# The tail of a transformer block's backward pass: the input gradient's sum and copy on ScalarE, and another order for the last group's wqkv gradient

## The chip, the cores and the metric

The kernel runs on one core of a Trainium2 chip. A core has TensorE for matrix products, VectorE, ScalarE and GpSimd for the rest, and SyncE, which here only issues DMAs. The metric is the device time of one execution in microseconds, as the median of several runs.

## The reference

A block with attention and a gated feed-forward part, side by side on one normalised input, and all its gradients. The sequence has 2048 rows of 448 values, 16 heads of 28, and a feed-forward width of 1792; inputs and outputs are bf16.

```python
def _A_ref(x, wqkv, wo):                      # attention, H = 16, Dh = 28
    qkv = (x @ wqkv).reshape(B, S, 3, H, Dh)  # -> q, k, v per head
    p = softmax(q @ k.T * Dh ** -0.5)
    return (p @ v).reshape(B, S, D) @ wo

def _B_ref(x, w_gate, w_up, w_down):
    return (silu(x @ w_gate) * (x @ w_up)) @ w_down

def _fwd_reference(...):
    xn = _layernorm(x, axis=-1)
    return x + _A_ref(xn, A_wqkv, A_wo) + _B_ref(xn, B_w_gate, B_w_up, B_w_down)

out, vjp = jax.vjp(_fwd_reference, A_x, A_wqkv, A_wo, B_w_gate, B_w_up, B_w_down)
return (out, *vjp(grad_out))
```

The last step of the backward pass concerns us. With g the gradient with respect to the normalised row xn, the gradient of the input row is `rstd * (g - mean(g) - xn * mean(g * xn)) + grad_out`: it needs two sums per row, of g and of g times xn.

## The kernel before

The order of all instructions is written out by hand: each engine executes its own instructions in the order in which the program lists them, and a framework adds the waits between engines. There are three stages.

The first stage runs the forward attention for four groups of four heads, and lets TensorE do feed-forward products in between. The second runs the backward attention in 512 units of a query tile and a key block; per unit ScalarE computes `E` (L808), VectorE `ds` (L814), and SyncE's queue transposes `ds` by DMA. In between it computes the output rows, the feed-forward's part of the input gradient (in two summands, into `pA_d` and `pB_d`), and the wqkv gradient of groups 0 to 2 (jobs of kind `dwq`).

The third stage, the tail (L849 to L905), is what the change touches. It has this order:

- DMA loads: `dy_t` (the whole output gradient, ScalarE's queue, L854), four loads of `pab` (the feed-forward's parts of the input gradient, two halves each of `pA_d` and `pB_d`, L858), and the first `dq_c` loads (L864), all on SyncE's queue but the first. A `dq_c` tile holds the gradients of q, k and v for two row tiles of 128 rows, 768 KB; there are three buffers, and `load_c(t // 2 + 2)` is issued ahead of every even row tile, behind the stores of the row tiles before it.
- The wqkv gradient of the last group, for four blocks `c` of its 448 rows (128, 128, 128 and 64). `dwq_mms` gives 64 products for each block: 32 for keys and values (`kvm`, L622, from `dkv_sp`), then 32 for queries (`qm`, L627, from `dq_sp`). `dwq_out` copies the block on ScalarE (L637), rearranges it in six GpSimd copies (L644) and stores it (L645). The last `dq_sp` half comes from the transposition (L757) of `dq_o` (L753), the very last result of the second stage.
- 16 row tiles of the input gradient. TensorE adds the two `pab` parts by an identity matrix (L880) and 12 products of `dq_c` with `wq` (L882) into one PSUM bank, `g_ps`. Three PSUM tiles named `sd` rotate over the wqkv blocks and these row tiles. Then, per row tile: VectorE copies `g_ps` to `g_sb` and sums it in the same pass (`s1`, L886); VectorE multiplies `g_sb` by `xn` and sums (`junk`, `s2`, L890); two operations on one value per row make `bb` (L894) and `cc` (L896); ScalarE computes `t1 = rstd * g_sb + bb` (L899); VectorE computes `t2 = xn * cc + t1` (L901; the profile prints both `t1` and `t2` as `t`); GpSimd adds `dy_t` (`dx`, L904); SyncE's queue stores (L905).

Of the kernel before, what the change touches and what calls it, by code (L numbers as in the profile page):

```python
# [9 lines left out]
ACT = mybir.ActivationFunctionType  # L10
ALU = mybir.AluOpType
AX = mybir.AxisListType
FP32 = mybir.dt.float32
BF16 = mybir.dt.bfloat16
# [4 lines left out]
D = 448  # L19
# [5 lines left out]
P = 128  # L25
NT = S // P
# [11 lines left out]
def kernel(  # L38
# [19 lines left out]
    pe, act, dve, pool, sp = nc.tensor, nc.scalar, nc.vector, nc.gpsimd, nc.sync  # L58
# [27 lines left out]
    rstd = const.tile([P, NT], FP32, name="rstd")  # L86
    rl_all = const.tile([P, NT, H], FP32, name="rl_all")
    xn_sp = const.tile([P, NT, DP], BF16, name="xn_sp")
# [40 lines left out]
    for c, (d0, dn) in enumerate(DCH):  # L129
        pool.tensor_copy(  # L130
            out=wq_sb[:dn, c].rearrange("p t g (hh r) -> p t (g hh) r", r=HP)[:, :, :, :DH],
            in_=wst[:dn, c, :].rearrange("p (t h d) -> p t h d", t=3, h=H))
# [4 lines left out]
    for hh in range(4):  # L137
        pool.dma_start(out=wo_pad[HP * hh:HP * hh + DH, :, :D], in_=wo_v[hh])
    dve.tensor_reduce(
        out=r_ones[:], in_=ident_f[:].rearrange("p (a b) -> p a b", b=HP)[:, :, 28:30],  # L140
# [49 lines left out]
    for b in range(5):  # L190
        if b < 4:
            bs = slice(4 * b, 4 * b + 4)
            for i in range(4):
                t = 4 * b + i
# [4 lines left out]
            for i in range(4):  # L199
                t = 4 * b + i  # L200
                dve.tensor_scalar(out=xn_sp[:, t, :D], in0=x_b[b][:, i, :],
                                  scalar1=mv[:, t, 0:1], scalar2=rstd[:, t:t + 1],
                                  op0=ALU.subtract, op1=ALU.mult)
# [4 lines left out]
        if b > 0:  # L208
            for tq in range(3):
                m = proj_unit(0, tq, b - 1, "act" if tq == 0 else "dve")  # L210
# [32 lines left out]
    for b in range(4):  # L243
        sp.dma_start_transpose(
            out=dyT[:, 4 * b:4 * b + 4].rearrange("p t c s -> p (t c) s"),
            in_=dy_sp[:, 4 * b:4 * b + 4, :].rearrange("p t d -> p (t d)"))
# [309 lines left out]
    ps_sd = cst.enter_context(tc.tile_pool(name="ps_sd", bufs=3, space=PSUM))  # L556
# [58 lines left out]
    def dwq_mms(g, c, ps):  # L615

        out = []
        lhs = lambda t: xn_sp[:, t, c * P:(c + 1) * P]

        def kvm(t):  # L620
            for hp in range(2):
                pe.matmul(ps[:, hp * P:(hp + 1) * P], lhsT=lhs(t), rhs=dsp[2 * g + hp][0][:, t, :],  # L622
                          start=(t == 0 and hp == 0), stop=(t == NT - 1), skip_group_check=True)

        def qm(t):
            for hp in range(2):
                pe.matmul(ps[:, 256 + hp * 64:256 + hp * 64 + 64], lhsT=lhs(t),  # L627
                          rhs=dsp[2 * g + hp][1][:, t // 8, t % 4, t % 8 // 4, :],
                          start=False, stop=(t == NT - 1), skip_group_check=True)
        for f in (kvm, qm):  # L630
            out += [lambda t=t, f=f: f(t) for t in range(NT)]
        return out

    def dwq_out(g, c, ps):
        d0, dn = DCH[c]
        o = outp.tile([P, 384], BF16, name="dwq_raw")
        act.copy(out=o[:], in_=ps[:, :384])  # L637
        z = outp.tile([P, 3, 4, DH], BF16, name="dwq_z")
        kv = o[:, :256].rearrange("p (h v j r) -> p h v j r", h=2, v=2, r=HP)
        for tq in range(3):  # L640
            for hp in range(2):
                src = (o[:, 256 + 64 * hp:320 + 64 * hp].rearrange("p (j r) -> p j r", r=HP) if tq == 0
                       else kv[:, hp, 2 - tq])
                pool.tensor_copy(out=z[:, tq, 2 * hp:2 * hp + 2, :], in_=src[:, :, :DH])  # L644
        pool.dma_start(  # L645
            out=out_2[d0:d0 + dn, :].rearrange("p (t c) -> p t c", t=3)[:, :, g * 4 * DH:(g + 1) * 4 * DH],
            in_=z[:dn].rearrange("p t h d -> p t (h d)"))

    def job_mms(i, ps):
        j = jobs[i]  # L650
        if j[0] == "dwq":
            return dwq_mms(j[1], j[2], ps)
        if j[0] == "y":
            t, x = chunk[i]
            out = []
            for n in range(NFC + G):
                rhs = (wo_pad[:, n, :D] if n < G else wtile["wd"][:, n - G, :])
                out.append(lambda n=n, rhs=rhs: pe.matmul(ps[:, :D], lhsT=t[:, n, :], rhs=rhs,  # L658
                                                          start=(n == 0), stop=False))
            out.append(lambda: pe.matmul(ps[:, :D], lhsT=ident_bf[:], rhs=x[:], start=False, stop=True))  # L660
            return out
        t = chunk[i]
        w = wtile[("wg", "wu")[j[1]]]
        return [lambda n=n: pe.matmul(ps[:, :D], lhsT=t[:, n, :], rhs=w[:, n, :],  # L664
                                      start=(n == 0), stop=(n == NFC - 1)) for n in range(NFC)]
# [106 lines left out]
    for k in range(N + 2 * UW):  # L772
# [36 lines left out]
        if 1 <= k <= N:  # L809
# [5 lines left out]
            if qi not in TQ:  # L815
                sp.dma_start_transpose(out=dsT[:, :, :, qi * P:(qi + 1) * P].rearrange("p j c q -> p (j c) q"),
                                       in_=DS[k - 1][:].rearrange("p j c -> p (j c)"))
# [8 lines left out]
        if pos == 1 and job:  # L826
            st["aux"] = ps_x.tile([P, 512], FP32, name="aux")
            fillers = job_mms(W, st["aux"])
# [20 lines left out]
    with ExitStack() as fin:  # L849
        ckf = fin.enter_context(tc.tile_pool(name="ckf", bufs=3))  # L850
        wk = fin.enter_context(tc.tile_pool(name="wk", bufs=3))
        one = fin.enter_context(tc.tile_pool(name="one", bufs=1))
        dy_t = one.tile([P, NT, D], BF16, name="dy_t")
        act.dma_start(out=dy_t[:], in_=dy_d)  # L854
        pab = [one.tile([P, NT, D], BF16, name=f"pab{i}") for i in range(2)]
        for i, src in enumerate((pA_d, pB_d)):
            for hf in range(2):
                sp.dma_start(out=pab[i][:, 8 * hf:8 * hf + 8, :], in_=src[:, 8 * hf:8 * hf + 8, :])  # L858
        dq_c = {}

        def load_c(ck):
            if ck < NT // 2:
                dq_c[ck] = ckf.tile([P, 3 * G, 2 * P], BF16, name="dq_c")
                sp.dma_start(out=dq_c[ck][:], in_=dqkv_d[ck])  # L864
        load_c(0)
        load_c(1)
        for c in range(4):
            ps = ps_sd.tile([P, 2, 512], FP32, name="sd")
            for f in dwq_mms(3, c, ps[:, 0, :]):
                f()  # L870
            dwq_out(3, c, ps[:, 0, :])
        wq = wtile["wq"]
        for t in range(NT):
            if t % 2 == 0:
                load_c(t // 2 + 2)
            cks = dq_c[t // 2]
            g_t = ps_sd.tile([P, 2, 512], FP32, name="sd")
            g_ps = g_t[:, 0, :D]
            for i in range(2):
                pe.matmul(g_ps, lhsT=ident_bf[:], rhs=pab[i][:, t, :], start=(i == 0), stop=False)  # L880
            for n in range(3 * G):
                pe.matmul(g_ps, lhsT=cks[:, n, (t % 2) * P:(t % 2 + 1) * P], rhs=wq[:, n, :],  # L882
                          start=False, stop=(n == 3 * G - 1))
            g_sb = wk.tile([P, D], FP32, name="g_sb")
            s1 = wk.tile([P, 1], FP32, name="s1")
            dve.tensor_scalar(out=g_sb[:], in0=g_ps, scalar1=1.0, scalar2=None, op0=ALU.mult, op1=ALU.add,  # L886
                              accum_out=s1[:])
            junk = wk.tile([P, D], FP32, name="junk")
            s2 = wk.tile([P, 1], FP32, name="s2")
            dve.scalar_tensor_tensor(out=junk[:], in0=g_sb[:], scalar=1.0, in1=xn_sp[:, t, :D],  # L890
                                     op0=ALU.mult, op1=ALU.mult, accum_out=s2[:])
            bb = wk.tile([P, 1], FP32, name="bb")
            cc = wk.tile([P, 1], FP32, name="cc")
            dve.scalar_tensor_tensor(out=bb[:], in0=s1[:], scalar=-1.0 / D, in1=rstd[:, t:t + 1],  # L894
                                     op0=ALU.mult, op1=ALU.mult)
            dve.scalar_tensor_tensor(out=cc[:], in0=s2[:], scalar=-1.0 / D, in1=rstd[:, t:t + 1],  # L896
                                     op0=ALU.mult, op1=ALU.mult)
            t1 = wk.tile([P, D], FP32, name="t1")
            act.activation(out=t1[:], in_=g_sb[:], func=ACT.Identity, scale=rstd[:, t:t + 1], bias=bb[:, 0:1])  # L899
            t2 = wk.tile([P, D], FP32, name="t2")  # L900
            dve.scalar_tensor_tensor(out=t2[:], in0=xn_sp[:, t, :D], scalar=cc[:, 0:1], in1=t1[:],  # L901
                                     op0=ALU.mult, op1=ALU.add)
            dx = wk.tile([P, D], BF16, name="dx")
            pool.tensor_tensor(out=dx[:], in0=t2[:], in1=dy_t[:, t, :], op=ALU.add)  # L904
            sp.dma_start(out=out1_d[:, t, :], in_=dx[:])  # L905
# [31 lines left out]
```

## Time and profile before

| what | before |
|---|---|
| median of 3 runs | 1739.35 us (1738.14 to 1739.54) |
| the profiled execution's own time | 1738.91 us |
| its span in the profile | 1737.1 us |
| busy share of the span: TensorE, VectorE, ScalarE, GpSimd | 87%, 63%, 72%, 23% |
| last `dq_o` on VectorE, the second stage's last result | 1653.98 us |
| first product of `dq_c` with `wq` | 1675.71 us |
| first `t1` and last `t1` on ScalarE | 1679.60 and 1729.04 us |
| end of the last `dx` on GpSimd | 1731.69 us |

Times are microseconds from the span's start, durations of single operations microseconds or nanoseconds. A timeline row has the start, the busy time, the engine, the line of the program, the operation, what it writes and reads, the shapes, and in brackets how long the engine was idle before it and whose end released it. The chain of waits is the work that ended last, followed back from the end: each piece is what the next one waited for. Busy shares are averages over the three stages; the tail is the last 5% of the span and has to be read by itself.

### The profile page before, as it was taken

The page shows a single profiled execution, that of the slowest core. Times are in us where ns is not written, and L with a number is a line of the kernel's source. Part 1 is how long each engine was busy: PE and PEld are TensorE (multiplying, and loading weights), DVE is VectorE, ACT ScalarE, POOL GpSimd, SP SyncE. Part 2 cuts the span into 40 slices and gives each one's busy share as a digit, 9 for nine tenths or more (in the row PEclk, how much of TensorE's full clock was granted, in tenths as well). Part 3 has the DMA queues.
Part 4 walks back from the last instruction along what each step waited for, and adds up shares of the span by engine and source line. Part 5 has one row for each costly group of instructions (what it writes and reads, how often), then busy time and mean ns, then how long its engine had stood idle before and what let it go on. Part 6 is the DMA issues. An engine that isn't in the chain of part 4 may idle for free.

```text
span 1737.1 us, 31931 instructions
## 1 busy us (share of the span) xinstructions
PE 1504.9 (87%) x12176; PEld 590.4 (34%) x12176; DVE 1103.0 (63%) x1402; ACT 1242.1 (72%) x1346; POOL 400.8 (23%) x664
## 2 busy tenths in 40 slices
PE   3799999999999998868888888888888888888885
PEld 2132333333233332223333334333334333433352
DVE  5365555565555454527777767777777777777726
ACT  2497888888777776637777767777777877777711
POOL 4132334343333342420001011110102101111122
PEclk9699999999899999889999989999999999999988
DMA  3794758775866585659999799998999999899873
GB/s 122 149 184 96 160 115 177 142 141 124 173 142 122 106 171 111 135 168 218 202 188 202 143 193 185 178 202 178 205 185 184 209 170 171 156 176 177 168 236 102
DMA packets 682153, 285.11 MB, mean 164 GB/s; under 512 B 637792, under 2 KB 651088, under 8 KB 682000
## 3 DMA queue, kind: packets, MB, share of 16 engines
q1 hardware_dynamic: 653616, 215.74, 65.9%
q0 software_dynamic: 25808, 64.30, 14.6%
q10 hardware_dynamic: 2576, 3.04, 0.6%
q8 instruction: 95, 1.56, 0.4%
q14 instruction: 58, 0.48, 0.1%
HBM read 67.34 MB, written 63.44 MB: 75 GB/s over the span
## 4 chain that ended last, share of the span: by engine, by line
PE 63%; ACT 16%; DMA 6%; DVE 6%; issue 6%; SPq 1%; POOL 1%; ACTq 0%; DVEq 0%; POOLq 0%
PE s_ps L531 9%; PE f_ps L339 9%; PE f_ps L313 8%; ACT E L808 7%; ACT dsT L722 7%; PE aux L664 5%; PE o_ps L511 4%; PE sd L793 4%; PE aux L735 4%; PE aux L658 3%; PE aux L721 3%; PE f_ps L157 3%; PE acc L694 3%; PE sd L803 2%; DMA dsT<-ds 2%
## 5 line engine op out<-in xcount | busy, mean ns | idle before, releaser
L814 DVE TENSOR_TENSOR ds<-sd,E 128x1024 bf16<-128x1024 f32 x512 | 624.3, 1223 | 231.1 <-PE sd L803 209.8
L808 ACT ACTIVATE E<-sd 128x1024 bf16<-128x1024 f32 x512 | 518.5, 1027 | 176.0 <-PE sd L803 153.9
L535 ACT ACTIVATE eT<-s_ps 128x1024 bf16<-128x1024 f32 x512 | 517.9, 1024 | 158.5 <-PE s_ps L531 153.0
L803 PE MATMUL sd<-KV,QD 32*128 32x512 bf16 x1024 | 202.4, 388 | 61.2 <-ACT E L808 60.2
L793 PE MATMUL sd<-KV,QD 32*128 32x512 bf16 x1024 | 201.9, 391 | 7.7 <-DMA KV<-kT_d 7.6
L694 PE MATMUL acc<-E,dOsp 128*32 128x512 bf16 x1024 | 204.4, 396 | 0.6 <-ACT dkv_o L700 0.5
L531 PE MATMUL s_ps<-qT,kT 32*128 32x512 bf16 x1024 | 204.7, 397 | 0.0
L694 PE MATMUL acc<-ds,Qsp 128*32 128x512 bf16 x1024 | 204.6, 396 | 0.0
L722 ACT COPY dsT<-aux 128x1024 bf16<-128x1024 bf16 x128 | 129.5, 1012 | 47.9 <-PE aux L721 46.2
L339 PE MATMUL f_ps<-xnT,wgu 128*128 128x512 bf16 x448 | 137.2, 404 | 24.7 <-DVE w_sb L365 12.9
L378 POOL DMA_DIRECT2D hd_d<-fT x168 | 126.9, 769 | 39.2 <-DVE fT L363 25.4
L531 PEld LDWEIGHTS <-kT 32*128 32x128 bf16 x1024 | 48.3, 91 | 204.2 <-issue 201.9
L664 PE MATMUL aux<-W,ck 128*128 128x448 bf16 x448 | 101.0, 353 | 14.2 <-ACT dsT L722 14.2
L313 PE MATMUL f_ps<-xn_sp,f_sp 128*128 128x448 bf16 x448 | 110.6, 356 | 0.0
L803 PEld LDWEIGHTS <-QD 32*128 32x128 bf16 x1024 | 66.5, 91 | 105.6 <-issue 101.9
L511 PE MATMUL o_ps<-eT,v_sp 128*32 128x512 bf16 x1024 | 102.0, 400 | 0.0
L709 POOL DMA_DIRECT2D dqkv_d<-dkv_o x64 | 39.1, 616 | 271.1 <-ACT dkv_o L700 271.0
L793 PEld LDWEIGHTS <-QD 32*128 32x128 bf16 x1024 | 48.3, 91 | 138.2 <-issue 122.9
L735 PE MATMUL aux<-dsT,Ksp 128*32 128x512 bf16 x1024 | 75.2, 387 | 22.4 <-ACT dsT L722 18.1
L694 PEld LDWEIGHTS <-dOsp 128*32 128x32 bf16 x1024 | 50.7, 93 | 118.8 <-issue 118.7
L721 PE MATMUL aux<-ident_bf,ds 128*128 128x128 bf16 x1024 | 80.3, 222 | 12.3 <-DVE dq_acc L750 6.9
L351 DVE SCALAR_TENSOR_TENSOR g<-t_sb,f_ps 128x512 f32<-128x512 f32 x56 | 38.4, 686 | 65.1 <-ACT t_sb L349 64.9
(129 smaller groups left out, 1731.1 us busy)
## 6 DMA issues: line engine op xcount, KB each, us to landing
hd_d<-fT POOLq DMA_DIRECT2D x168, 128.0 KB, 4.3
ck<-hd_d SPq DMA_DIRECT2D x32, 448.0 KB, 4.2
ck<-hd_d SPq DMA_DIRECT2D x16, 576.0 KB, 4.7
dsT<-ds SPq DMA_TRANSPOSE x384, 3.9
dq_c<-dqkv_d SPq DMA_DIRECT2D x8, 768.0 KB, 4.6
dqkv_d<-dkv_o POOLq DMA_DIRECT2D x64, 64.0 KB, 3.1
W<-wT_d SPq DMA_DIRECT2D x14, 224.0 KB, 3.9
out_dram<-dw_o POOLq DMA_DIRECT2D x28, 96.0 KB, 3.8
```

What stands on the lines that cost most here:

```text
L313: pe.matmul(acc[:, :D], lhsT=src[:, 12 * (t // 4) + 4 * wi + t % 4, :], rhs=rhs[:, t, :D], start=(t == 0), stop=(t == NT - 1))
L339: pe.matmul(st[name][:], lhsT=w(c), rhs=src[:, tsl, c, :], start=(c == 0), stop=(c == 3))
L511: pe.matmul(o_ps[HP * hh:HP * (hh + 1), :], lhsT=v[:, kt, HP * hh:HP * (hh + 1)], rhs=e[hh // 2][:, hh % 2, :], start=(kt == 0), stop=(kt ...
L531: pe.matmul(s_ps[:, j, :], lhsT=kT[r:r + HP, kt * P:(kt + 1) * P], rhs=qT[r:r + HP, qc * 512:(qc + 1) * 512], start=True, stop=True, tile_ ...
L535: act.activation(out=e[:], in_=s_ps[:], func=ACT.Exp, scale=SCALE)
L664: return [lambda n=n: pe.matmul(ps[:, :D], lhsT=t[:, n, :], rhs=w[:, n, :], start=(n == 0), stop=(n == NFC - 1)) for n in range(NFC)]
L694: pe.matmul(acc[r:r + HP, :], lhsT=src[:, qt, 64 * hp + HP * j:64 * hp + HP * j + HP], rhs=m[:, j, :], start=(qt == 0), stop=(qt == NT - 1 ...
L722: act.copy(out=dsT[:, :, :, qi * P:(qi + 1) * P].rearrange("p j c q -> p (j c) q"), in_=ps[:])
L793: pe.matmul(s_ps[:, j, :], lhsT=q[HP * j:HP * j + HP, qt * P:(qt + 1) * P], rhs=kv[HP * j:HP * j + HP, kc * 512:(kc + 1) * 512], start=Tru ...
L803: pe.matmul(d_ps[:, j, :], lhsT=q[r:r + HP, qt * P:(qt + 1) * P], rhs=kv[r:r + HP, kc * 512:(kc + 1) * 512], start=True, stop=True, tile_p ...
L808: act.activation(out=E[k][:], in_=s_ps[:], func=ACT.Exp, scale=SCALE)
L814: dve.tensor_tensor(out=DS[k - 1][:], in0=d_ps[:], in1=E[k - 1][:], op=ALU.mult)
```

## The change

The wqkv gradient of the last group: `dwq_mms` returns the keys' and values' products and the queries' products as two lists. The tail first runs the keys' and values' products of all four row blocks, then the queries' products block by block, each followed by its `dwq_out`. For that the four blocks lie two by two in the two banks of two `sd` tiles, where each block had its own `sd` tile before. The jobs in the second stage keep their order.

The input gradient: the pass that copies and sums `g_ps` goes from VectorE to ScalarE (an Identity activation with `accum_out`), and its copy `g_sb` is bf16. `junk` and `t1` read `g_ps` in PSUM instead of `g_sb`. VectorE has 16 instructions fewer in the program's order and ScalarE 16 more; DMAs, products and GpSimd's work stay the same in number.

```diff
         for f in (kvm, qm):
-            out += [lambda t=t, f=f: f(t) for t in range(NT)]
+            out.append([lambda t=t, f=f: f(t) for t in range(NT)])
         return out
...
         if j[0] == "dwq":
-            return dwq_mms(j[1], j[2], ps)
+            return sum(dwq_mms(j[1], j[2], ps), [])
...
         load_c(0)
         load_c(1)
+        mms = []
         for c in range(4):
-            ps = ps_sd.tile([P, 2, 512], FP32, name="sd")
-            for f in dwq_mms(3, c, ps[:, 0, :]):
-                f()
-            dwq_out(3, c, ps[:, 0, :])
+            if c % 2 == 0:
+                g_t = ps_sd.tile([P, 2, 512], FP32, name="sd")
+            mms.append((g_t[:, c % 2, :], dwq_mms(3, c, g_t[:, c % 2, :])))
+        for part in range(2):
+            for c, (ps, m) in enumerate(mms):
+                for f in m[part]:
+                    f()
+                if part == 1:
+                    dwq_out(3, c, ps)
...
-            g_sb = wk.tile([P, D], FP32, name="g_sb")
+            g_sb = wk.tile([P, D], BF16, name="g_sb")
             s1 = wk.tile([P, 1], FP32, name="s1")
-            dve.tensor_scalar(out=g_sb[:], in0=g_ps, scalar1=1.0, scalar2=None, op0=ALU.mult, op1=ALU.add,
-                              accum_out=s1[:])
+            act.activation(out=g_sb[:], in_=g_ps, func=ACT.Identity, accum_out=s1[:])
             junk = wk.tile([P, D], FP32, name="junk")
             s2 = wk.tile([P, 1], FP32, name="s2")
-            dve.scalar_tensor_tensor(out=junk[:], in0=g_sb[:], scalar=1.0, in1=xn_sp[:, t, :D],
+            dve.scalar_tensor_tensor(out=junk[:], in0=g_ps, scalar=1.0, in1=xn_sp[:, t, :D],
                                      op0=ALU.mult, op1=ALU.mult, accum_out=s2[:])
...
-            act.activation(out=t1[:], in_=g_sb[:], func=ACT.Identity, scale=rstd[:, t:t + 1], bias=bb[:, 0:1])
+            act.activation(out=t1[:], in_=g_ps, func=ACT.Identity, scale=rstd[:, t:t + 1], bias=bb[:, 0:1])
```

## The prediction

> **What bounds the kernel now.** The change lies wholly in the tail, after the last attention gradient, so the page was read first for its end: the span is 1737.1 us, this execution's own time 1738.91 us (1.81 us lie outside the span), and the median of the three runs, 1739.35 us, is 0.44 us more. The sum below is made against 1738.91. About 0.2%, 3.5 us, is what a measurement can tell from no change.
>
> The second view is the chain of waits that ended last, where the tail begins.
>
> ```profile
> 1659.07 16.60 DMA dq_c<-dqkv_d
> 1675.66 0.05 issue
> 1675.71 2.46 PE sd L882 x12
> 1678.17 0.02 issue
> 1678.19 0.64 DVE g_sb L886 x2
> ```
>
> The first `dq_c` load takes 16.60 us because it queues behind `dy_t` and four `pab` loads, with the DMA engines full. TensorE stands waiting when it lands. The timeline of TensorE shows that the wqkv gradient ends before that:
>
> ```profile
> 1653.88 3.26 PE L622 MATMUL sd<-dkv_sp,xn_sp 128*128 128x128 bf16 x32
> 1662.36 0.96 PE L627 MATMUL sd<-dq_sp,xn_sp 128*128 128x64 bf16 x15 [4.74 <-DMA dq_sp<-dq_o]
> 1663.13 3.60 PE L622 MATMUL sd<-dkv_sp,xn_sp 128*128 128x128 bf16 x32
> ...
> 1672.13 1.10 PE L627 MATMUL sd<-dq_sp,xn_sp 128*128 128x64 bf16 x32
> 1673.07 0.54 PE L880 MATMUL sd<-pab,ident_bf 128*128 128x448 bf16 x2
> 1675.71 2.44 PE L882 MATMUL sd<-W,dq_c 128*128 128x448 bf16 x12 [2.10 <-DMA dq_c<-dqkv_d]
> ```
>
> There are two holes: 4.74 us for the last `dq_sp` transposition, and 2.10 us for `dq_c`. Only the second is on the path.
>
> Then the 16 tiles follow. VectorE's timeline, with those of ScalarE and GpSimd, gives one period:
>
> ```profile
> 1690.14 0.69 DVE L901 SCALAR_TENSOR_TENSOR t<-xn_sp,cc,t 128x448 f32<-128x448 bf16 x1 [0.83 <-ACT t L899]
> 1690.74 0.62 DVE L886 TENSOR_SCALAR_CACHE_REDUCE g_sb<-sd 128x448 f32<-128x448 f32 x1
> 1691.40 1.02 DVE L890 SCALAR_TENSOR_TENSOR junk<-g_sb,xn_sp 128x448 f32<-128x448 f32 x1
> 1692.35 0.15 DVE L894 SCALAR_TENSOR_TENSOR bb<-s,rstd 128x1 f32<-128x1 f32 x1
> 1693.45 0.69 DVE L901 SCALAR_TENSOR_TENSOR t<-xn_sp,cc,t 128x448 f32<-128x448 bf16 x1 [0.83 <-ACT t L899]
> ```
>
> ```profile
> 1692.60 0.76 ACT L899 ACTIVATE t<-g_sb,bb,rstd 128x448 f32<-128x448 f32 x1 [2.55 <-DVE bb L894]
> ```
>
> ```profile
> 1690.91 1.03 POOL L904 TENSOR_TENSOR dx<-t,dy_t 128x448 bf16<-128x448 f32 x1 [2.28 <-DVE t L901]
> ```
>
> VectorE is a ring: `t2` to `g_sb` 0.60, `g_sb` to `junk` 0.66, `junk` to `bb` 0.95, `bb` to `t1` on ScalarE 0.25, `t1` to `t2` 0.85; sum 3.31 us. From the first `t1` (1679.60) to the last (1729.04) it is 49.44 us for 15 periods. TensorE needs 2.65 us per tile (1678.37 to 1681.02) and is ahead. So VectorE with its wait for ScalarE sets the tail.
>
> `junk` is the row to look at. In the first tile, with GpSimd idle, it took 0.62; here `dx` runs from 1690.91 to 1691.94, and `junk` ends 0.48 after `dx`. It is held, not slowed. `g_sb`, which reads PSUM, overlaps `dx` too and keeps its 0.62.
>
> **The change, part by part.** (1) VectorE loses `g_sb`: 0.66 per period. ScalarE gets it. A plain ScalarE copy of 128x448 out of PSUM to bf16 took 0.527 (`row_o`, L673). What writing out the sum adds is in no row: VectorE's own read of its sum took 0.08, the smallest ScalarE operation (128x4, L197) 0.30, and no cost is the bound below. I take 0.15, between the two, so 0.68 with it. Nobody reads the new bf16 `g_sb`.
>
> (2) In the changed program's waits, `junk` waits for ScalarE, not for TensorE: the two passes over the same sums run one after the other. Here a rule speaks against the change. The Trainium skill, PSUM — Partial Sum Buffer, "PSUM bank collisions raise a hardware error", says that two engines must not read one bank at a time, so the pass that went to ScalarE can't lie beside `junk`; no run here shows a collision. By it the first tile gives the +0.06 below; side by side it would be about -0.5, and the sum 1733.4 instead of 1734.0.
>
> In steady state most of it hides. ScalarE starts it when `t1` of the tile before ends, while VectorE runs `t2`. From a `t1` start: 0.76, then 0.68, then 0.05 to `junk`, 1.49; VectorE is free at 0.85 + 0.60 = 1.45. So 0.04 shows. Were it not hidden, it would cost 0.73 a period. Queued behind `g_sb` on ScalarE is only its own tile's `t1`, which must wait for `junk` anyhow; behind the waiting `junk` on VectorE are `bb`, `cc` and `t2` of the same tile.
>
> In the first tile it shows fully: 0.04 + 0.68 + 0.05 + 0.55 + 0.19 = 1.51 from TensorE's end to `t1`, against 1.45 now. +0.06, between -0.09 and +0.21.
>
> (3) `junk` now reads PSUM and one SBUF tile. Bounds: 0.62 as alone, or held by `dx` as now. I take 0.62: `ds` (L814) has just these kinds of operands and took 1.23 us at 1037.80, across GpSimd's copies of 1037.47 to 1038.54, as it does without them.
>
> (4) `bb` and `cc` keep two SBUF inputs, and now start earlier, inside `dx`. Free, the ring is 1.49 + 0.55 + 0.25 = 2.29, less than TensorE's 2.65. Held, they go at the end of `dx`: from there 0.18 to `t1` (the short value of `bb` to `t1`, as part of `bb` is done by then), 0.85 to `t2`, 0.77 to `dx`, 1.03 for `dx`: 2.83. No row shows a 128x1 operation under `dx`; the nearest is `junk` itself, the same instruction with both inputs in SBUF, which is held. I take 2.83. The skill's page SBUF — State Buffer, "Who interferes with whom", makes no exception for small operands: two SBUF inputs contend with a GpSimd instruction that reads SBUF. By it the sum is 1734.0, by the bare 0.15 of the `bb` row 1731.5.
>
> `t1` out of PSUM I leave at 0.76; a lower bound is 0.59 (`t_sb`, 128x512 out of PSUM), by which TensorE's 2.65 would rule.
>
> (5) 15 periods: the first three have `t1` to `t2` 0.06 shorter (fewer waits), so 3 x 2.77 + 12 x 2.83 = 42.27. Gain 49.44 - 42.27 = 7.17.
>
> (6) The reordered gradient. The keys' and values' parts run through the 4.74 us hole: 1653.88 + 3.26 + 3 x 1.95 gives 1663.0, after `dq_sp` landed (1662.36). Then four queries' parts of about 1.0, of which the second and fourth wait some 0.6 for ScalarE's copy of the other half of their tile: done near 1668.4 instead of 1673.1. What hides it: `dq_c` lands at 1675.66 as before, since SP issues the same loads in the same order. GpSimd's copies and stores of the four blocks (84 KB each) come at most some 4 us earlier; at the 400 GB/s of that stretch each is 0.2 us of DMA, so `dq_c` moves by no more than 0.4. The gain is nothing; the wait grows from 2.1 to over 7 us.
>
> And that wait costs. The windows view shows the granted clock:
>
> ```profile
> 1660.00:1663.40 3.40, 1.04 (x18) 1.03 (x18) 0.00 (x0) 0.00 (x0) 0.00 (x0) 0.51 1.12 367
> 1663.40:1666.80 3.40, 3.40 (x37) 3.40 (x35) 0.00 (x0) 0.48 (x1) 1.79 (x7) 0.50 1.01 402
> 1666.80:1670.20 3.40, 3.40 (x90) 3.40 (x88) 0.00 (x0) 0.48 (x1) 1.48 (x7) 0.99 1.03 411
> ```
>
> Each row has the stretch, its length, busy time and count of TensorE, its weight loads, VectorE, ScalarE and GpSimd, then the clock, the DMA share and GB/s. After the 4.74 us hole it was 0.50, and back at 0.99 some 4.5 us after work began. After the 2.10 us hole it stayed at 1.00. Now the hole in front of `dq_c` is the long one, with one or two `pab` products in it, so tile 0 starts at half clock. Price, from the same rows: 15 queries' products 0.96 instead of 0.52, 32 of 3.60 instead of 1.95, 32 of 1.26 instead of 1.10: 2.25 us. On tile 0 it is fully on the path. Bounds: 0, and 3.4 if the half clock lasts 6.8 us.
>
> Sum: -7.17 + 0.06 + 2.25 = -4.86, 1738.91 - 4.86 = 1734.0.
>
> `dq_c` for later tiles is issued behind the store of `dx` two tiles back: 0.45 + 4.6 to land + two tiles of products 5.1 + 3.9 to the end of `dx` = 14.1 for six tiles, against 6 x 2.83 = 17.0: hidden, until landing takes 7.5.
>
> **The rivals.** *TensorE becomes the bound*: `bb` and `cc` aren't held (or `t1` is quicker), period 2.65. 49.44 - 15 x 2.65 = 9.69; -9.69 + 2.31 = -7.4, 1731.5. For it: they are 128x1. Against: the held `junk`.
>
> *The clock holds*: -2.25 off either, 1731.8 or 1729.3. Against: both idle stretches of 3 us or more (before 1652.05 and 1662.36) were followed by half clock.
>
> *Slower: `junk` still collides with `dx`*, though one input is in PSUM. It now starts within 0.1 us of `dx`. If `junk` is first, `dx` starts at 1.49 + 0.55 = 2.04 and ends at 3.07, `bb` is held till then: 3.25. If `dx` is first (1.62 to 2.65), `junk` ends 0.48 later: 2.65 + 0.48 + 0.25 = 3.38. Over 15 periods -0.9 or +1.1, with the 2.31 of the start: 1740.3 to 1742.3, and 1743.5 with the longer half clock. It decides from a period of 3.15 up. Against it: `g_sb` and `ds` rows.
>
> *The reorder alone does what the words say*: impossible as a gain while `dq_c` lands at 1675.66; it is inside the sum at zero.
>
> **How the numbers follow.** Forecast 0.50, 1734.0, with own bounds 1731.8 (no half clock) to 1735.2. TensorE's bound 0.22, 1731.5. Clock holds 0.10, 1729.3 to 1731.8. `junk` collides 0.10, 1740.3 to 1743.5. Left, 0.08: late `dq_c` and the unseen, around 1737 to 1740. The range from 1729.0 to 1737.0 leaves out `junk`'s collision and most of the rest. Faster by over 0.2% (under 1735.9) 0.79, within 0.2% 0.14, slower 0.07.
>
> **What would show it.** `junk` at 0.62 in all tiles; `bb` and `cc` ending just after `dx`; `t1` starts 2.83 apart; over 7 us with only `pab` products before tile 0; clock 0.50 after 1675.7. I'm wrong if `junk` stays at 1.0, if the ring is 2.65 or over 3.1, if `dq_c` lands earlier, or if tile 0's products take 2.4 us.

## The result and the profile after

The changed kernel takes 1730.32 us (median of 22 runs, 1725.21 to 1739.99), the kernel before in the same sessions 1737.39 us (22 runs, 1731.33 to 1744.15). The ratio is 0.9963, 95% interval 0.9949 to 0.9978: faster by 0.2 to 0.5%. The forecast of 1734.0 stands for a ratio of 1734.0 / 1738.91 = 0.9972, inside the interval, and 1730.32 lies in its range of 1729.0 to 1737.0. The medians differ by 7.07 us.

The profiled execution took 1725.21 us with a span of 1723.4 us, 13.7 us less than the one before. This is not all the change's work: the last `dq_o` on VectorE, ahead of everything that was changed, already ends at 1647.24 instead of 1654.67 us, 7.43 us earlier. Over the fourteen profiled executions of this study, whose programs are all alike up to there, that end lies anywhere from 1647.24 to 1656.61 us. So the profiles are compared from that point on. I call the stretch from the end of the last `dq_o` to the end of the last `dx` the tail: 77.02 us before, 70.75 us after, a gain of 6.27 us. A second pair of profiles of the two kernels gave 77.78 and 70.61 us, a gain of 7.17 us. So the tails alone account for the difference of the medians, and the 7.43 us ahead of them are the scatter of single executions.

The chain of waits that ended last, after, at the start of the row tiles:

```profile
1652.11 16.71 DMA dq_c<-dqkv_d
1668.82 0.04 issue
1668.86 4.21 PE sd L888 x12
```

The first `dq_c` load is as long as before (16.71 against 16.60), and the 12 products behind it take 4.21 us where they took 2.46. TensorE's timeline has the reorder and its price:

```profile
1646.45 7.32 PE L622 MATMUL sd<-dkv_sp,xn_sp 128*128 128x128 bf16 x128
...
1659.25 1.09 PE L627 MATMUL sd<-dq_sp,xn_sp 128*128 128x64 bf16 x32 [0.64 <-ACT dwq_raw L637]
...
1664.57 0.53 PE L886 MATMUL sd<-pab,ident_bf 128*128 128x448 bf16 x1 [4.03 <-DMA pab<-pB_d]
1668.86 4.21 PE L888 MATMUL sd<-W,dq_c 128*128 128x448 bf16 x12 [3.77 <-DMA dq_c<-dqkv_d]
```

All 128 products of keys' and values' parts now run in one piece, and the last queries' part waits 0.64 us for ScalarE's copy of the other half of its tile. TensorE is done with the wqkv gradient at 1660.3, and then stands for 4.03 and 3.77 us with one `pab` product in between. The windows view has the granted clock as the third number from the end (before the DMA share and GB/s), here for two microseconds out of tile 0 and tile 1:

```profile
1671.00:1672.00 1.00, 1.00 (x4) 0.44 (x3) 0.00 (x0) 0.00 (x0) 0.00 (x0) 0.50 0.12 49
1673.00:1674.00 1.00, 1.00 (x7) 0.50 (x6) 0.22 (x1) 0.64 (x2) 0.00 (x0) 1.00 0.00 0
```

Four products in a microsecond at clock 0.50, seven at 1.00: tile 0 runs at half clock, tile 1 at full.

One late period, from the timelines of VectorE, ScalarE and GpSimd:

```profile
1710.74 0.68 DVE L906 SCALAR_TENSOR_TENSOR t<-xn_sp,cc,t 128x448 f32<-128x448 bf16 x1 [0.85 <-ACT t L904]
1711.34 0.62 DVE L895 SCALAR_TENSOR_TENSOR junk<-sd,xn_sp 128x448 f32<-128x448 f32 x1
...
1711.88 0.67 DVE L899 SCALAR_TENSOR_TENSOR bb<-s,rstd 128x1 f32<-128x1 f32 x1
1712.47 0.14 DVE L901 SCALAR_TENSOR_TENSOR cc<-s,rstd 128x1 f32<-128x1 f32 x1
```

```profile
1709.91 0.72 ACT L904 ACTIVATE t<-sd,bb,rstd 128x448 f32<-128x448 f32 x1 [1.48 <-DVE cc L901]
1710.54 0.53 ACT L892 ACTIVATE g_sb<-sd 128x448 bf16<-128x448 f32 x1
1710.96 0.20 ACT L892 ACTIVATION_READ_ACCUMULATOR g_sb<-sd 128x1 f32 x1
1712.64 0.72 ACT L904 ACTIVATE t<-sd,bb,rstd 128x448 f32<-128x448 f32 x1 [1.48 <-DVE cc L901]
```

```profile
1711.50 1.03 POOL L909 TENSOR_TENSOR dx<-t,dy_t 128x448 bf16<-128x448 f32 x1 [1.70 <-DVE t L906]
```

`junk` is back at 0.62 although `dx` runs from 1711.50 to 1712.53. `bb`, on one value per row, takes 0.67 and ends at 1712.55, 0.02 after `dx`: it is held. So it goes in every tile from the fifth on: `bb` starts ever earlier inside `dx`, its length grows from 0.15 in the first tile to 0.67, and it ends within 0.02 of `dx`'s end. The new ring goes through GpSimd: `dx`'s end to `t1` 0.11, `t1` to `t2` 0.83, `t2` to `dx` 0.76, `dx` 1.03, together 2.73 us against 3.31 before.

### The profile page after: what moved, and what is told of

Same layout as the page of the kernel before. It is cut to its first block, busy times and chain, and to the rows that moved or that the text cites. A ratio compares the mean times of both kernels' runs of the same rounds, so it can differ in the third digit from the quotient of the medians.

```text
span 1723.4 us, 31944 instructions
## 1 busy us (share of the span) xinstructions
PE 1494.2 (87%) x12176; PEld 586.3 (34%) x12176; DVE 1092.3 (63%) x1370; ACT 1251.4 (73%) x1378; POOL 400.8 (23%) x664
## 3 DMA queue, kind: packets, MB, share of 16 engines
q10 hardware_dynamic: 2576, 3.04, 0.6%
## 4 chain that ended last, share of the span: by engine, by line
PE 61%; ACT 16%; DMA 7%; DVE 6%; issue 5%; SPq 2%; POOL 1%; ACTq 0%; DVEq 0%; POOLq 0%
PE s_ps L531 9%; PE f_ps L313 8%; PE f_ps L339 8%; ACT E L808 7%; ACT dsT L722 7%; PE aux L664 5%; PE o_ps L511 4%; PE sd L793 4%; PE aux L735 4%; PE aux L658 3%; DMA dsT<-ds 3%; PE f_ps L157 3%; PE aux L721 3%; PE acc L694 2%; PE sd L803 2%
```

## The experiments

The theory: the gain is the shorter ring, held up by `dx` over `bb`; the reorder brings nothing and costs the half clock at tile 0; what sets the start of the tiles is the `dq_c` load. The rivals: the reorder has a share in the gain; the clock would have dropped anyway; the ring's length comes from something else than `dx`. All times in the table are from the profiles, in us; ratios are against the kernel before. "Start" is the time from the last `dq_o`'s end to the first `dq_c` product, "tile 0" the duration of its 12 products, "ring" the mean of the last five periods. In brackets are the names of the runs, by which the expectations call them.

| kernel | ratio, 95% interval | tail | start | tile 0 | ring |
|---|---|---|---|---|---|
| before | 1 | 77.02 | 21.04 | 2.44 | 3.31 |
| before, second profile | | 77.78 | 21.78 | 2.44 | 3.31 |
| after | 0.9963, 0.9949 to 0.9978 | 70.75 | 21.62 | 4.21 | 2.73 |
| after, second profile | | 70.61 | 21.63 | 4.08 | 2.73 |
| ScalarE part alone (`e1_scalar_only`) | 0.9949, 0.9931 to 0.9968 | 71.31 | 22.29 | 3.79 | 2.73 |
| reorder alone (`e2_reorder_only`) | 0.9998, 0.9980 to 1.0015 | 80.01 | 21.86 | 4.61 | 3.31 |
| `bb`, `cc` with one data input (`e3_free_small`) | 0.9955, 0.9935 to 0.9974 | 73.11 | 24.97 | 3.95 | 2.65 |
| `junk` from SBUF (`e4_junk_sbuf`) | 0.9979, 0.9964 to 0.9995 | 77.95 | 23.32 | 4.66 | 3.04 |
| TensorE kept busy (`e5_warm`) | one run, 1727.62 | 71.36 | 24.04 | 2.43 | 2.73 |
| `dq_c` ahead of half the `pab` (`e6_loads`) | 0.9914, 0.9890 to 0.9937 | 65.88 | 16.84 | 3.72 | 2.73 |
| the same, without reorder (`e7_loads_noreorder`) | 0.9922, 0.9905 to 0.9940 | 66.88 | 19.53 | 2.43 | 2.73 |
| `e6_loads`, `dy_t` late, free `bb` (`e9_loads_dy`) | 0.9902, 0.9882 to 0.9923 | 62.02 | 13.68 | 2.43 | 2.65 |
| and a third `dq_c` early (`e10_best`) | 0.9884, 0.9862 to 0.9905 | 60.44 | 13.26 | 2.43 | 2.65 |
| the last without reorder (`e11_best_oldorder`) | 0.9881, 0.9858 to 0.9903 | 58.98 | 12.08 | 2.44 | 2.65 |

### The two parts, each alone

The first kernel is the one before with the ScalarE edits only:

```diff
-            g_sb = wk.tile([P, D], FP32, name="g_sb")
+            g_sb = wk.tile([P, D], BF16, name="g_sb")
...
-            dve.tensor_scalar(out=g_sb[:], in0=g_ps, scalar1=1.0, scalar2=None, op0=ALU.mult, op1=ALU.add,
-                              accum_out=s1[:])
+            act.activation(out=g_sb[:], in_=g_ps, func=ACT.Identity, accum_out=s1[:])
...
-            dve.scalar_tensor_tensor(out=junk[:], in0=g_sb[:], scalar=1.0, in1=xn_sp[:, t, :D],
+            dve.scalar_tensor_tensor(out=junk[:], in0=g_ps, scalar=1.0, in1=xn_sp[:, t, :D],
...
-            act.activation(out=t1[:], in_=g_sb[:], func=ACT.Identity, scale=rstd[:, t:t + 1], bias=bb[:, 0:1])
+            act.activation(out=t1[:], in_=g_ps, func=ACT.Identity, scale=rstd[:, t:t + 1], bias=bb[:, 0:1])
```

> The kernel before with ScalarE's sum and copy alone; the wqkv gradient keeps its old order. Tail here means from the end of the last dq_o on VectorE to the end of the last dx on GpSimd: 77.0 us before, 70.75 us after. Theory (the ring gives the gain, the reorder costs a start at half clock): the ring is 2.73 us as after, tile 0's 12 products take 2.44 us and not 4.21, so the tail is 68.4 to 69.2 us, some 1.8 us less than after. Rival (the reorder helps or is free): the tail is 70.7 us or more.

The second is the one before with the reorder only:

```diff
...
-            for f in dwq_mms(3, c, ps[:, 0, :]):
-                f()
-            dwq_out(3, c, ps[:, 0, :])
...
+        for part in range(2):
+            for c, (ps, m) in enumerate(mms):
+                for f in m[part]:
+                    f()
+                if part == 1:
+                    dwq_out(3, c, ps)
```

> The kernel before with the reordered wqkv gradient alone; VectorE keeps sum and copy. Theory: dq_c lands as before, TensorE waits over 7 us for it, tile 0 starts at half clock, the ring is 3.31 us; the tail is 78.5 to 79.5 us, 1.5 to 2.5 us slower than before, about 0.1% of the time. Rival (the hole of 4.74 us was worth something): the tail is 77.0 us or less.

The ScalarE part alone has the whole gain (0.9949 of the time before) and the same ring of 2.73 us; the reorder alone has none that can be told (0.9980 to 1.0015). That settles where the gain comes from. The reorder alone has a tail of 80.01 us, 0.5 more than expected. That is 3.0 longer than before: 2.17 from tile 0 at half clock, 0.82 from a later start. But the ScalarE part alone did not get the tail of 68 to 69 us that the theory wanted. It got 71.31, which by the number is on the rival's side. Its TensorE timeline and windows say why:

```profile
1672.06 3.79 PE L882 MATMUL sd<-W,dq_c 128*128 128x448 bf16 x12 [2.33 <-DMA dq_c<-dqkv_d]
```

```profile
1672.00:1673.00 1.00, 0.94 (x5) 0.51 (x6) 0.00 (x0) 0.00 (x0) 0.00 (x0) 1.00 1.01 417
1673.00:1674.00 1.00, 1.00 (x4) 0.45 (x3) 0.00 (x0) 0.00 (x0) 0.51 (x4) 0.50 0.70 272
```

The order of the kernel before, and a wait of only 2.33 us, and the clock still falls to 0.50, about a microsecond after TensorE has begun again. So the half clock is not the reorder's alone, and the rival isn't needed for the 71.31: with tile 0 at 2.44 and no slow start of tile 1 (the first period is 2.99, against 2.66 in the changed kernel) the tail would have been 69.6, and the start was 0.67 later than in the changed kernel. The reorder makes the wait for `dq_c` 8 us instead of 2, and the half clock came with it every time instead of now and then.

To see how often that happens without a change, both unchanged kernels were profiled once more.

> The kernel before, unchanged, for a second profiled execution. In the first the clock stayed at 1.00 after the hole of 2.10 us, while in e1_scalar_only, which has the same order of loads and products up to tile 0, it fell to 0.50 for 3 us after a hole of 2.33 us. If the half clock depends on the reorder alone, tile 0's products take 2.44 us here; if it comes by chance of timing, 2.4 to 4.2 us. The tail by dq_c's landing alone is 77 to 81 us.

> The changed kernel, unchanged, for a second profiled execution: ring 2.73 us, tile 0's products 3.9 to 4.7 us at half clock, dq_c's first product 21 to 25 us after dq_o, tail 70 to 74 us.

The kernel before waited 1.66 us for `dq_c` this time (2.10 before) and again kept its clock, 2.44 us for tile 0; the changed kernel needed 4.08. With the loads as they are in these two, every kernel with the reorder paid it (3.95 to 4.66 in five profiles), and without the reorder one of three did.

The traces show what decides. In all fourteen, every stretch between two steps of the granted clock is a whole multiple of 3.41 us (10.24 us at half clock in the changed kernel, from 1662.25 to 1672.49), so the steps lie on a grid, in another place in each execution. The windows view over single stretches of that grid, for the holes in question:

| profile | stretch of the grid, us | TensorE busy in it | clock in the next |
|---|---|---|---|
| before, hole of 2.10 | 1673.70 to 1677.11 | 1.40 | 1.00 |
| before, second profile, hole of 1.66 | 1674.13 to 1677.55 and 1677.55 to 1680.96 | 2.60 and 2.57 | 1.00 |
| ScalarE part alone, hole of 2.33 | 1669.58 to 1672.99 | 1.08 | 0.50 |
| after | 1658.84 to 1662.25 | 1.28 | 0.50 |
| after, second profile | 1661.79 to 1665.20 | 1.39 | 0.50 |

Of the stretches at full clock that lie wholly in the tails of the fourteen profiles, the same limit divides all: after 1.39 us busy or less the next one is at 0.50, after 1.40 or more at 1.00. (It is a limit for these products; earlier in the program, with products of other shapes, the clock fell after a stretch with 2.18 us busy, 1636.59 to 1640.00 in the second profile of the kernel before.) So the length of the hole isn't what counts, but how it lies on the grid: 1.66 us were cut in two and harmless, and the kernel before kept its clock by a hundredth of a microsecond. The clock comes back at a step of the grid too, and the price is half of the time that the products run until then: in the changed kernel (1672.49 - 1668.86) / 2 = 1.8, measured 1.77.

### Does idling lower the clock?

The changed kernel, with 20 products of no use (into a tile of their own) after each of tile 0's two `pab` products, while it waits for `pab` and `dq_c`:

```diff
                 pe.matmul(g_ps, lhsT=ident_bf[:], rhs=pab[i][:, t, :], start=(i == 0), stop=False)
+                if t == 0:
+                    warm = ps_x.tile([P, 512], FP32, name="aux")
+                    for _ in range(20):
+                        pe.matmul(warm[:, :D], lhsT=ident_bf[:], rhs=xn_sp[:, 0, :D], start=True, stop=True)
```

> The changed kernel with 40 products of 128x448 that nobody reads (20 after each of tile 0's two pab products) to keep TensorE busy while it waits for dq_c. Theory (the idle stretch lets the clock fall): the clock stays at 1.00, tile 0's 12 products take 2.44 us and not 4.21, and from the first product of dq_c to the first t1 it is 3.9 us and not 5.66; the rest as after, so some 1.8 us less. Rival (the products of tile 0 are slow for another reason, such as the DMA traffic or late weights): 4.2 us as after. If dq_c lands earlier than in the other runs, the products before it may push tile 0 by up to some us.

```profile
1672.82 2.43 PE L892 MATMUL sd<-W,dq_c 128*128 128x448 bf16 x12
```

Tile 0 is at full clock, and from the first `dq_c` product to the first `t1` it takes 3.87 us instead of 5.66. The idling is the cause: the kernels of the next sections whose tile 0 follows other products without a wait have it at 2.43 or 2.44 too. In the tail as a whole it doesn't show (71.36), because the products of no use were themselves too many: the first `dq_c` was issued at 1653.70 and landed 16.7 us later, at 1670.4, 21.6 after `dq_o` as in the changed kernel, but the last of the 20 products ran until tile 0 began at 1672.82. That took back 2.4 us, more than the clock gave. The expectation had named this case.

### What holds the ring: the small operations, and `junk`

In the next kernel `bb` and `cc` take `rstd` as a scalar per row, not as a second data input:

```diff
-            dve.scalar_tensor_tensor(out=bb[:], in0=s1[:], scalar=-1.0 / D, in1=rstd[:, t:t + 1],
-                                     op0=ALU.mult, op1=ALU.mult)
+            dve.tensor_scalar(out=bb[:], in0=s1[:], scalar1=rstd[:, t:t + 1], scalar2=-1.0 / D,
+                              op0=ALU.mult, op1=ALU.mult)
```

> The changed kernel, with bb and cc as tensor_scalar: rstd is a per-partition scalar operand, so each has one tensor input in SBUF and not two. Theory (two SBUF inputs are what dx holds): bb takes 0.15 us in all tiles, the ring is under 2.65 us, TensorE sets the tile rate, t1 starts are 2.65 us apart; tail 69.6 us, 1.1 us less than after. Rival (bb is held for another reason, or any small operation is held): bb up to 0.67 us as after, ring 2.73 us, tail 70.7 us.

Its VectorE and GpSimd timelines:

```profile
1718.31 0.21 DVE L899 TENSOR_SCALAR bb<-s,rstd 128x1 f32<-128x1 f32 x1
```

```profile
1717.55 1.03 POOL L909 TENSOR_TENSOR dx<-t,dy_t 128x448 bf16<-128x448 f32 x1 [1.61 <-DVE t L906]
```

`bb` now starts and ends inside `dx` (1717.55 to 1718.58) in 0.21 us, in every tile, and the ring is 2.65, TensorE's own time per tile. So it was `dx` that held `bb`, through the second data input, and the first rival of the prediction is what happens without that hold. The tail didn't reach the 69.6 us expected, it is 73.11, since `dq_c` started 24.97 us after `dq_o` in this execution. The ring by itself is worth little: the last `t1` comes 40.07 us after the first, 0.78 less than in the changed kernel, and the interval of the ratio overlaps that of the changed kernel.

The other test gives `junk` its second SBUF input back:

```diff
-            dve.scalar_tensor_tensor(out=junk[:], in0=g_ps, scalar=1.0, in1=xn_sp[:, t, :D],
+            dve.scalar_tensor_tensor(out=junk[:], in0=g_sb[:], scalar=1.0, in1=xn_sp[:, t, :D],
```

> The changed kernel, but junk reads ScalarE's bf16 g_sb in SBUF instead of PSUM, so it has two SBUF inputs. Theory (dx holds what has two SBUF inputs, or is held by it): junk and dx collide in full, ring 3.2 to 3.4 us, tail 77 to 80 us, so nearly all of the gain is gone. Rival (taking g_sb off VectorE gave the gain, where junk reads from makes no difference): ring 2.73 us, tail 70.7 us.

The timeline of VectorE and GpSimd together:

```profile
1692.19 0.62 DVE L895 SCALAR_TENSOR_TENSOR junk<-g_sb,xn_sp 128x448 f32<-128x448 bf16 x1
...
1692.35 1.35 POOL L909 TENSOR_TENSOR dx<-t,dy_t 128x448 bf16<-128x448 f32 x1 [1.70 <-DVE t L906]
...
1692.73 0.98 DVE L899 SCALAR_TENSOR_TENSOR bb<-s,rstd 128x1 f32<-128x1 f32 x1
```

Here `junk` starts first and keeps its 0.62; it is `dx` that is held, 1.35 instead of 1.03, and then `dx` holds `bb` for 0.98, until 1693.7. The ring is 3.04. The mechanism is the one expected, its size was put too high (3.2 to 3.4). From the first to the last `t1` it is 45.90 us, 5.05 more than in the changed kernel, and the ratio goes back to 0.9979. The Trainium skill, SBUF — State Buffer, section "Who interferes with whom", says that issue order decides who blocks; both orders are now in the rows: `dx` first and `bb` held to 0.67, `junk` first and `dx` held to 1.35. In the second tile of the same run `dx` started first, at 1683.11, and `junk` was held to 1.44.

### What sets the start of the tiles

The wait for `dq_c` is the largest thing left. This kernel changes the order of the loads only: `load_pab(hf)` loads half `hf` of both parts, and only the first eight row tiles' halves stay ahead of `dq_c`.

```diff
-        for i, src in enumerate((pA_d, pB_d)):
-            for hf in range(2):
+        def load_pab(hf):
+            for i, src in enumerate((pA_d, pB_d)):
                 sp.dma_start(out=pab[i][:, 8 * hf:8 * hf + 8, :], in_=src[:, 8 * hf:8 * hf + 8, :])
+        load_pab(0)
...
         load_c(1)
+        load_pab(1)
```

> The changed kernel with its loads in another order on SyncE's queue: the first halves of both pab tiles, then two dq_c, then the second halves of pab (needed from tile 8 on). Theory (dq_c is late only because 3.6 MB of pab and 1.8 MB of dy_t go ahead of it, and the reorder has a value only once that is gone): the first product of dq_c comes at the end of the wqkv gradient, 13 to 15 us after dq_o instead of 21.6, with no long hole and no half clock; tail 60 to 64 us, 6 to 10 us less than after. Rival (dq_c waits for something else, such as the store of the last dq_o): it comes at 20 us or more, and the tail stays near 70.

> ScalarE's sum and copy, the old order of the wqkv gradient, and the loads as in e6_loads. Theory: with dq_c early the wqkv gradient sets the start, and its hole for dq_sp is on the path, so that tile 0 starts some 4 to 5 us later than in e6_loads (18 to 19 us after dq_o); tail 65 to 68 us. Rival (the reorder is worth nothing in any case): the same tail as e6_loads.

With the reorder `dq_c` is there 16.84 us after `dq_o`, not the 13 to 15 expected: `dy_t`, 1.8 MB on ScalarE's queue, still moves ahead of it, as the run with `dy_t` moved shows below. The tail of 65.88 misses the 60 to 64 expected, but the time falls to 0.9914. Tile 0 is at half clock again, after one `pab` product between waits of 1.21 and 1.75 us:

```profile
1669.72 3.72 PE L891 MATMUL sd<-W,dq_c 128*128 128x448 bf16 x12 [1.75 <-DMA dq_c<-dqkv_d]
```

The second kernel has the same loads without the reorder. Now TensorE never waits for `dq_c`; the hole that the kernel before had off the path, the one for the last `dq_sp`, is on it:

```profile
1662.77 0.96 PE L627 MATMUL sd<-dq_sp,xn_sp 128*128 128x64 bf16 x15 [5.14 <-DMA dq_sp<-dq_o]
```

The first `dq_c` product comes 2.7 us later than with the reorder, but at full clock, and the two tails differ by 1.0 us; the ratios can't be told apart.

Then `dy_t` goes from ScalarE's queue to SyncE's, in four pieces behind the first `dq_c` loads, with the free `bb` and `cc` in it; and in a further kernel the third `dq_c` load comes ahead of `dy_t` too, since tile 4 had waited 1.77 us for it:

```diff
-        act.dma_start(out=dy_t[:], in_=dy_d)
...
         load_c(1)
+        load_c(2)
+        for b in range(0, NT, 4):
+            sp.dma_start(out=dy_t[:, b:b + 4, :], in_=dy_d[:, b:b + 4, :])
         load_pab(1)
...
-            if t % 2 == 0:
+            if t % 2 == 0 and t > 0:
                 load_c(t // 2 + 2)
```

> e6_loads, and bb and cc with one SBUF input as in e3_free_small, and dy_t in four parts on SyncE's queue behind the two dq_c. Theory: start as e6_loads or up to 1 us sooner, as less goes ahead of dq_c, and a ring of 2.65 us set by TensorE; tail 59 to 62 us, 1.0 to 2 us less than e6_loads, and 0.8% less time than the kernel before. Rival (the loads that were moved back are now late for tiles 0 to 8): dx of the first tiles or the pab products wait, and the tail is not shorter than in e6_loads.

> e9_loads_dy with the third dq_c load also ahead of dy_t (in e9_loads_dy tile 4 waited 1.77 us for it, behind the second halves of pab). Theory: that wait goes, from the first to the last t1 it is 39.8 us (41.8 in e9_loads_dy), tail 59.5 to 61 us, up to 2 us less than e9_loads_dy. Rival: dy_t is now late for the first dx and the time is the same.

These give 0.9902 and 0.9884, with tails of 62.02 (the upper end of what was expected) and 60.44; the start at 13.68 and 13.26 is even earlier than the 15.8 to 16.8 that the first was given. In both, tile 0 follows the wqkv gradient without a wait and at full clock. The last run takes the reorder out of the better one. If the reorder is needed to keep the `dq_sp` hole off the path, the tail must get longer by most of that hole.

> e10_best without the reordered wqkv gradient. It tells what the reorder is worth once dq_c is early. Theory: the hole for dq_sp, 4 to 5.5 us, is on the path again; tile 0 starts 4 to 5 us later than in e10_best and the tail is 64 to 66 us. Rival, from e6_loads against e7_loads_noreorder, which differ by 1.0 us in the tail: at most 2 us.

It lost nothing: 0.9881, with the shortest tail of all, 58.98 us. That expectation fell, and the timeline shows why:

```profile
1657.86 1.10 PE L627 MATMUL sd<-dq_sp,xn_sp 128*128 128x64 bf16 x32
...
1667.42 2.44 PE L887 MATMUL sd<-W,dq_c 128*128 128x448 bf16 x12
```

There is no bracket in front of the queries' products: the hole is gone. The DMA view (line, queue, kind, count, median us from issue to landing) over the start of the tail has the reason, first before, then this kernel:

```profile
dq_sp<-dq_o SPq DMA_TRANSPOSE x2, 5.6
```

```profile
dq_sp<-dq_o SPq DMA_TRANSPOSE x2, 3.3
```

Each figure is the median of the two halves of the last `dq_sp`. The last half, which TensorE waits for, took 7.6 to 11.5 us in the eleven profiles with `dy_t` on ScalarE's queue and 2.9 to 3.3 in the three with `dy_t` behind it on SyncE's queue. The first half, issued some 3 to 5 us earlier, differs little (3.6 to 5.8 and 3.1 to 5.4). The order of the other loads is not the reason: with `dq_c` ahead of half the `pab` and `dy_t` left where it was, the last half took 8.3 and 8.4; and the free `bb` comes only later. `dy_t` used to start ahead of it (1654.02 before, on the other queue) and to move beside it. So the hole that the reorder fills was made by the load of `dy_t`; with that load out of the way, there is nothing to fill.

## Why the prediction was right

The mechanism of the ring was right, and so was the reorder's worth of nothing; the sum was too small, and the total hides it. The sum was -4.86 us; the tails of the profiled pair differ by 6.27 us, of the second pair by 7.17, the medians by 7.07. The ratio would put 1738.91 at 0.9963 x 1738.91 = 1732.5, within the forecast's own bounds of 1731.8 to 1735.2; the plain time of 1730.32 lies below them, as the kernel before turned out 1.5 us faster over 22 runs than the execution that the sum started from. By the time alone two rivals fit better, TensorE as the bound (1731.5) and the clock that holds (1729.3 to 1731.8). The rows rule both out: the ring is 2.73 and not 2.65, and the clock fell. By its own steps:

| step | forecast | measured in the tail |
|---|---|---|
| 15 periods, first to last `t1` | 42.27, -7.17 | 40.85, -8.59 |
| TensorE's end to `t1` in tile 0 | +0.06 | 0.00 (1.45 both) |
| tile 0 at half clock | +2.25 | +1.77 |
| landing of the first `dq_c` | 0 | +0.58 |
| last `t1` to the end of `dx` | 0 | -0.03 |
| sum | -4.86 | -6.27 |

- **The ring** was right in its mechanism, down to who holds whom: `bb` waits for `dx`, and the cycle runs through GpSimd. Its term was mis-sized by 1.42 us, most of the error. Of the 0.10 us per period, 0.07 is the step from `dx`'s end to `t1` (0.11 instead of 0.18, as the held `bb` ends 0.02 after `dx`), the rest is 0.02 and 0.01 less in the two steps after it. The first two periods, 2.66 and 2.64, were TensorE's, which the forecast had at 2.77. `t1` out of PSUM took 0.72, not 0.76.
- **ScalarE's sum** came out as a second instruction of 0.20 us, but it starts 0.42 after the first one: together they take 0.62 (1710.54 to 1711.16; 0.62 to 0.64 over the tiles), less than the 0.68 forecast. So the first tile lost nothing instead of 0.06. Between `t1` and `junk` it is hidden as worked out: `junk` starts right behind `t2` in the row shown.
- **`junk`** at 0.62 in all tiles was right, and the rival that it still collides did not happen. The experiment that forced it gave a period of 3.04, below the 3.25 and 3.38 that the rival priced: it had `bb` go only after a full `dx` behind `junk`, while the run shows `dx` beginning inside `junk` and held only 0.32.
- **The reorder** is worth nothing, as the sum had it: alone it is 0.9998. The queries' waits of 0.62 and 0.64 for ScalarE's copies were as forecast. That the last `dq_sp` would have landed before the queries' part was not: TensorE waited 1.10 us for it, off the path.
- **The half clock** came, near the price given. Its cause was drawn too narrowly: the prediction put all of it down to the reorder, because the kernel before had kept its clock after a hole of 2.10 us. That was luck, by the busy time of 1.40 against 1.39 above; the ScalarE part alone lost its clock after 2.33. So the two parts can't be billed apart as the sum did, and taking the reorder out would not have won 2.25 us: the interval of the ScalarE part alone overlaps that of the whole change.
- **The landing of `dq_c`** was taken as fixed. In the profiles with these loads it varies from 21.04 to 24.97 us after `dq_o` with nothing changed that bears on it, twice as much as all other errors of the sum together (2.0 us). That it moved by only 0.58 between the two profiles, against the other errors, is luck. The chances had only 0.08 for it.

What stays open is why the landing of `dq_c` varies so much, and what counts as busy for the clock with products of other shapes.

## What to carry to other kernels

Move a pass off the engine that sets a ring, and then follow the ring anew: here it went from VectorE to GpSimd's `dx`, and a 128x1 operation with two SBUF inputs was enough to tie the two engines together. Before reordering work to fill a hole, ask which transfer makes the hole: the loads' order and queue, with the free `bb`, took the ratio from 0.9963 to 0.9884, twice as much again as the change itself brought, and left the reorder nothing to fill. Where executions differ by 7 us ahead of the edit, size a 0.3% change stage by stage in the profile, and the total only by many runs.

## What the runs showed of the hardware

- The granted clock stepped only on a grid of 3.41 us, in another place in each execution. In the tails of the fourteen profiles it fell to 0.50 after every stretch of the grid with TensorE busy for 1.39 us or less, and after none with 1.40 or more. So it fell after waits much shorter than the prediction's 3 us (2.33 us, or 1.21 and 1.75 us with one product between), about a microsecond after work had begun again, and stayed at 1.00 after 2.10 and 1.66 us. Where it fell, it cost tile 0 1.3 to 2.2 us. The Trainium skill, TensorE: Matmul & The Clock Gate, "Part 1: The HAM clock gate", speaks of an activity window of some 3.4 us that runs freely; these traces agree.
- A VectorE operation on 128 values with two inputs in SBUF is held by a GpSimd operation as one of 128x448 is: `bb` took 0.15 without and 0.67 under `dx`. With one input in PSUM (`junk`, 0.62), or with the second one as a scalar per row (`bb`, 0.21), it isn't.
- ScalarE's sum is an instruction of its own of 0.19 to 0.20 us, which starts 0.42 to 0.44 us after an activation of 0.53 to 0.55 has begun: the pair took 0.62 to 0.64.
- A small DMA transposition (half of the last `dq_sp`) took 7.6 to 11.5 us beside the 1.8 MB load of `dy_t` on another queue, against 2.9 to 3.3 with that load behind it on the same queue.
